# A causal filter and a spectral mix on one core: x two rows to a partition, the filter in twelve products per head on quarters of the array

## The chip, the cores and the metric

The kernel runs on one core of a Trainium2 chip. The metric is the device time of one execution in microseconds (us), of which the median over several runs is taken. The profile is of one further execution. Engines: TensorE (PE, with its weight loads PEld), VectorE (DVE), ScalarE (ACT), GpSimd (POOL) and SyncE (SP).

## The reference

`x` has 8 batches of 3264 rows and 192 channels. Eight heads of 24 channels each are filtered along the rows with a causal filter of 7 taps (a softmax of `weight`); the result is called c below. Of c the first 64 Fourier modes along the rows are taken, each is multiplied by a complex 192 x 192 matrix of its own, and they are transformed back to y. The output is u + relu(u @ w_ch) with u = c + y.

```python
out = np.einsum('hk,bskhg->bshg', softmax(weight), windows_of(x_pad))   # 7 taps, 8 heads of 24 channels
X = np.fft.rfft(c, axis=1)[:, :64]
Y = X @ (w_r + 1j * w_i)                                                # one matrix a mode
u = c + np.fft.irfft(Y, n=S, axis=1)
return u + np.maximum(u @ w_ch, 0)
```

Inputs and outputs are float32; x and the matrices are cast to bfloat16 while they are loaded.

## The kernel before, in words

**Layout.** The batches are taken in four pairs `q`. The 3264 rows of a batch are two halves of 1632; each half is six blocks (`NBH`) of 256 rows and a rest (`RR`) of 96. `xall[partition, q, t, k, d]` holds two tiles `t` of 128 rows to a block; row 128 t + p of a block lies on partition p, and `k` counts block, half and batch. `load_unit` (L169) issues one GpSimd transfer for each tile: 128 partitions, four rows of 192 float32 (768 B) each. `load_rest` (L179) loads the rests of all pairs, with some rows ahead of them.

**First stage.** A unit is one or two blocks of a pair: `UNITS` are blocks 4 and 5, blocks 2 and 3, and blocks 0 and 1 with the rest; the first pair has five smaller units (`UNITS0`). For a unit, `conv_pass` (L312) does the filter for two heads at a time: products of 128 rows of x (the moving side) with 64 columns of a band matrix (`band`, seen as `bd3`, one diagonal band of taps per head), which give every other row of c; `a` is the parity and `half` the tile. A second set of products adds the taps that reach into the tile or block before. The result, in a pair of PSUM banks from `next_pair` (three pairs in turn), is copied over x in `xall`, by ScalarE (three of four) or VectorE. So c lies with rows 2p + a of a block on partition p. A unit's filter also reads the block before its own, which the next unit loads.

`fold` (L348) makes the sum and the difference of the two halves on VectorE into `cpm`, and `dft` (L354) multiplies these with the table `ftab` (the cosines and sines, 128 columns) and adds up over the units of a pair in the bank `sums`. When a pair is done, `xtrans` (L372) transposes its spectrum into `xt`. The loop at L454 writes this order by hand: the filter of unit k, then the transform of unit k - 1, and in between one bank of transposes of c for the second stage (`some`, `c_bank`, L420: blocks of channels 0 to 127 of either batch, and channels 128 to 191 of both batches, each as a 64-wide transpose). After the loop come ten more such banks, the last transform, and the rest of the banks beside the mix. There are 42 banks (`tjobs`).

**The mix.** `mix` (L493) multiplies the spectrum of four modes at a time (`g`, 16 groups) with their matrices, on four column tiles of 32. The matrices come on GpSimd's queue behind x: groups 0 to 7 into places in `ct` that are still unused, groups 8 to 11 into `arena` when the filter's temporaries there are dead, groups 12 to 15 each into a place that the mix has just read (`load_w`, L299). The list at L827 (`beside`) says how many banks of transposes go beside each group; `beside_pair` puts some products of the second stage there, and `keep_busy` idle products.

**Second stage.** For each tile of 128 rows of c, `pieces` (L614) gives the products of either 64 rows of the array: three with the transposed c in `ct` (moving side `wa` and `wb`, halves of `w_ch`), and one with the inverse table `gtab` for y. `second_stage` (L743) plans them with fixed costs. ScalarE clamps, VectorE adds u, SyncE stores.

## Time and profile before

| | us |
|---|---|
| median of 3 runs | 175.84 (175.61 to 175.98) |
| the profiled execution | 175.52 |
| its span, first to last instruction | 173.7 |

| engine | busy us, share of the span | instructions |
|---|---|---|
| PE | 149.5 (86%) | 2837 |
| PEld | 127.8 (74%) | 2837 |
| DVE | 125.6 (72%) | 246 |
| ACT | 118.8 (68%) | 224 |
| POOL | 66.0 (38%) | 108 |

The transfers moved 40.85 MB, counted as they land. First come the loads of x and of the matrices on GpSimd's queue, at the end the stores on SyncE's. The mean granted clock of TensorE was 0.989.

How to read it: a row of a timeline has start and length in us, engine, line, operation, out<-in, shapes and count, and in brackets the idle time ahead of it with what ended it. A row of the windows has the stretch and its length, then busy time (and instructions) of PE, PEld, DVE, ACT and POOL, the granted clock, the DMA share and GB/s. A group has the count, then busy us and mean ns of one, then the idle time before. A wait has us in total, times, and the longest. A row of the transfers has their count, KB each and the median us from issue to landing.

### The profile page before, as it was taken

How to read it: one execution, taken by the hardware profiler on the slowest of the kernel's cores; microseconds unless marked ns; L12 is line 12 of the kernel's file. 1: busy time of each engine (PE TensorE's matmuls, PEld its weight loads, DVE VectorE, ACT ScalarE, POOL GpSimd, SP SyncE). 2: the span in 40 equal slices, each digit the busy share in tenths (PEclk: the TensorE clock that was granted, in tenths of full speed). 3: DMA queues.
4: the chain of work that ended last, by engine and by line, in shares of the span. 5: the costliest groups of instructions: out<-in, count | busy, mean ns of one | idle time of the engine just before them, and what ended most of it. 6: DMA issues, size and time to landing. Idle time of an engine off the chain costs nothing.

```text
span 173.7 us, 6647 instructions
## 1 busy us (share of the span) xinstructions
PE 149.5 (86%) x2837; PEld 127.8 (74%) x2837; DVE 125.6 (72%) x246; ACT 118.8 (68%) x224; POOL 66.0 (38%) x108
## 2 busy tenths in 40 slices
PE   0044898899999999799998899999999999999980
PEld 0043797789889889577865565788999988999950
DVE  3892868476778778675545542499998999999990
ACT  6369356658686686755874654588889899898850
POOL 7977997775775584344234300420000000000000
PEclk9999999999999999999999999999999999999995
DMA  2999999999999999999999996359969999999996
GB/s 17 166 173 189 193 188 191 191 189 192 191 190 191 192 204 206 206 206 206 207 208 206 207 205 115 88 191 389 388 233 396 351 357 383 337 339 385 386 356 196
DMA packets 51650, 40.85 MB, mean 235 GB/s; under 512 B 30020, under 2 KB 51524, under 8 KB 51620
## 3 DMA queue, kind: packets, MB, share of 16 engines
q0 software_dynamic: 36400, 20.06, 83.2%
q1 hardware_dynamic: 14948, 20.16, 32.5%
q8 instruction: 22, 0.36, 0.8%
q10 hardware_dynamic: 272, 0.20, 0.3%
q14 instruction: 8, 0.07, 0.1%
HBM read 39.62 MB, written 20.45 MB: 346 GB/s over the span
## 4 chain that ended last, share of the span: by engine, by line
DMA 46%; PE 37%; POOL 9%; issue 3%; DVE 1%; POOLq 0%; DVEq 0%
DMA xall<-in_x_dram 23%; PE outleft L644 18%; DMA arena<-in_moe_w_i_dram 13%; DMA ct<-in_moe_w_i_dram 11%; PE sumright L644 8%; PE mixright L644 8%; POOL xall L174 7%; DVE xall L712 1%; PE sumright L498 1%; PE trleft L429 1%; POOL loose L270 1%; PE sumright L818 0%; PE mixright L526 0%; PE mixright L548 0%; POOL arena L303 0%
## 5 line engine op out<-in xcount | busy, mean ns | idle before, releaser
L322 PEld LDWEIGHTS <-band 128*64 128x64 bf16 x944 | 38.7, 121 | 18.3 <-ACT band L241 11.1
L644 PEld LDWEIGHTS <-ct 64*128 64x128 bf16 x624 | 41.0, 94 | 4.8 <-PE trleft L644 0.5
L322 PE MATMUL cvleft<-xall,band 128*64 128x192 bf16 (+4 forms) x640 | 30.5, 248 | 13.9 <-ACT band L241 11.1
L644 PE MATMUL outleft<-mixa,gtab 64*128 64x384 bf16 x182 | 41.9, 323 | 0.1
L174 POOL DMA_DIRECT2D xall<-in_x_dram x48 | 36.0, 760 | 10.2 <-DMA xall<-in_x_dram 8.4
L644 PEld LDWEIGHTS <-gtab 64*128 64x128 bf16 x416 | 30.9, 94 | 3.0 <-PE outleft L644 1.1
L644 PE MATMUL outleft<-wa,ct 64*128 64x192 bf16 x208 | 30.4, 243 | 0.0
L351 DVE TENSOR_TENSOR arena<-xall 128x1536 bf16<-128x1536 bf16 (+1 forms) x28 | 22.4, 840 | 8.2 <-ACT xall L346 7.8
L690 ACT ACTIVATE outleft<-outleft 128x384 f32<-128x384 f32 x53 | 24.4, 477 | 4.6 <-PE outleft L644 2.3
L346 ACT CAST xall<-cvleft 128x768 bf16<-128x768 f32 (+3 forms) x29 | 21.4, 756 | 8.8 <-PE cvleft L322 7.3
L644 PE MATMUL sumright<-mixa,gtab 64*128 64x384 bf16 x92 | 25.8, 323 | 0.0
L644 PE MATMUL mixright<-mixa,gtab 64*128 64x384 bf16 x90 | 25.8, 323 | 0.0
L644 PE MATMUL outleft<-wb,ct 64*128 64x192 bf16 x104 | 23.3, 243 | 0.0
L398 DVE COPY ct<-trleft 128x1024 bf16<-128x1024 bf16 (+1 forms) x19 | 12.4, 662 | 12.7 <-PE trleft L429 7.8
L322 PE MATMUL cvright<-xall,band 128*64 128x192 bf16 (+4 forms) x304 | 15.9, 247 | 1.6 <-DVE xall L344 1.2
L396 ACT COPY ct<-trleft 128x1024 bf16<-128x1024 bf16 x13 | 13.2, 1012 | 4.6 <-PE trleft L426 2.4
L712 DVE TENSOR_TENSOR arena<-outleft,xall 128x384 f32<-128x384 f32 x27 | 14.4, 553 | 2.5 <-PE outleft L644 2.1
L346 ACT CAST xall<-cvright 128x768 bf16<-128x768 f32 (+3 forms) x13 | 9.8, 751 | 8.4 <-PE cvright L322 6.1
L644 PE MATMUL sumright<-wa,ct 64*128 64x192 bf16 x88 | 14.2, 243 | 0.0
L644 PE MATMUL mixright<-wa,ct 64*128 64x192 bf16 x80 | 13.8, 243 | 0.0
L426 PEld LDWEIGHTS <-xall 128*128 128x128 bf16 x208 | 11.7, 98 | 2.6 <-issue 0.3
L690 ACT ACTIVATE sumright<-sumright 128x384 f32<-128x384 f32 x26 | 12.3, 477 | 1.4 <-PE sumright L644 0.3
(147 smaller groups left out, 283.2 us busy)
## 6 DMA issues: line engine op xcount, KB each, us to landing
xall<-in_x_dram POOLq DMA_DIRECT2D x48, 192.0 KB, 7.9
out_dram<-arena SPq DMA_DIRECT2D x23, 384.0 KB, 4.0
out_dram<-xall SPq DMA_DIRECT2D x13, 384.0 KB, 4.1
out_dram<-ct SPq DMA_DIRECT2D x8, 384.0 KB, 4.6
ct<-in_moe_w_r_dram POOLq DMA_DIRECT2D x8, 288.0 KB, 9.4
ct<-in_moe_w_i_dram POOLq DMA_DIRECT2D x8, 288.0 KB, 10.4
arena<-in_moe_w_r_dram POOLq DMA_DIRECT2D x8, 288.0 KB, 10.5
arena<-in_moe_w_i_dram POOLq DMA_DIRECT2D x8, 288.0 KB, 10.9
```

The source lines that it names most:

```text
L174: nc.gpsimd.dma_start(out=xall[:, q, t % 2, k:k + 4, :], in_=src)
L270: nc.gpsimd.affine_select(out=dst, in_=dst, compare_op=ALU.not_equal, fill=fill, base=base, pattern=pattern, channel_multiplier=1)
L322: nc.tensor.matmul(o, bd3[:, h, c0:c0 + P - 1:2], xall[:, q, t, ks:ks + n, GRP * h:GRP * h + GRP], start=(main and a == 0), stop=not main, ...
L346: nc.scalar.copy(out=dst, in_=srcv)
L351: nc.vector.tensor_tensor(out=cpm[:, r, :, 0:2 * nb, :], in0=src[:, :, :, 0, :], in1=src[:, :, :, 1, :], op=op)
L396: nc.scalar.copy(out=out, in_=in_)
L398: nc.vector.tensor_copy(out=out, in_=in_)
L426: nc.tensor.transpose(o, cv[:, blk, 0:P], ident[:])
L429: nc.tensor.transpose(o[64 * i:64 * i + 64, :], cv[:, i, P:D], ident[:], tile_position=(0, 64 * i))
L644: m = nc.tensor.matmul((Z[s % NZ] if bank is None else bank)[:, cols], l, r, start=start, stop=stop, skip_group_check=True)
L690: act = nc.scalar.activation(out=z, in_=z, func=ACT.Relu)
L712: add = nc.vector.tensor_tensor(out=o[:, :, a, :], in0=Z[s % NZ][:, 0:2 * D].rearrange("p (i d) -> p i d", i=2), in1=c_rows(q, kk)[:, a, : ...
```

## The change

**x in memory.** x comes two rows to a partition: rows 2p and 2p + 1 of a block lie on partition p, next to each other, `xall[partition, q, k, t, d]` with `t` now the parity. A transfer is one half of one block of both batches, 128 partitions with two pieces of two rows (1536 B). The number of these transfers stays 48 of 192 KB; the rest's four shrink to 48 partitions for each pair. Rows that the filter needs ahead of the rest are moved from the last block by `rows_ahead`: four small products with a shift matrix (`ahead`) and four copies for each pair, ahead of its first unit.

**The filter.** `conv_head` does one head of a unit in one of six single banks (`next_bank`), in three steps of four products on the four 64 x 64 quarters of the array: equal parities (both at once, twice as wide), then odd into even, then even into odd. The products from the lower 64 rows are issued at once, those from the upper 64 rows six steps (two heads) later, after a `nop` that waits for the head's last lower product; then the bank is copied, by VectorE for heads 4 and 6, else by ScalarE. The band matrix has two parities of 129 columns per head. All pairs now have the three units of `UNITS`.

**The order.** `fold` of the unit before comes after head 1 of a unit; its transform after head 7. There are no transposes for the second stage in the filter's loop: the eight banks move beside the mix (`beside`).

**Second stage.** c of both batches lies side by side (`call`), so the transposes are three full blocks of 128 channels for two batches. Where 64 channels now lie on the other half of the partitions than in `wa`, their products use `wc`, `wa` with its halves swapped: two ScalarE copies ahead of the mix.

```diff
-    UNITS0 = ((5, 1, 0), (4, 1, 0), (3, 1, 0), (1, 2, 0), (0, 1, 1))
     UNITS = ((4, 2, 0), (2, 2, 0), (0, 2, 1))
-    units = [(q,) + u for q in range(NQ) for u in (UNITS if q else UNITS0)]
+    units = [(q,) + u for q in range(NQ) for u in UNITS]
...
+    call = xall[:, :, :, :, :].rearrange("p q (n i) t d -> p q n (i t d)", i=2).rearrange(
+        "p q n (t i d) -> p q n t i d", t=2, i=2)
...
-    cz = hand_out("left", "cv", (2, 2))
+    cz = hand_out("left", "cv", (1, 1, 1, 1))
...
-    cz += hand_out("right", "cv", (2,))
+    cz += hand_out("right", "cv", (1, 1))
...
+                k = 2 + 4 * b + 2 * h
+                src = bass.AP(tensor=x.tensor, offset=x.offset + (2 * q * S + HS * h + 2 * P * b) * D,
+                              ap=[[2 * D, P], [S * D, 2], [1, 2 * D]])
+                nc.gpsimd.dma_start(out=xall[:, q, k:k + 2, :, :].rearrange("p k t d -> p k (t d)"), in_=src)
...
+    def rows_ahead(q):
+        k = 2 + 4 * (NBH - 1)
+        for i in range(2):
+            z = next_bank()
+            for h in range(2):
+                nc.tensor.matmul(z[64 * (1 - h):64 * (1 - h) + R0, 0:2 * D], ahead[P - 32:P, :],
+                                 xall[P - 32:P, q, k + 2 * h + i, :, :].rearrange("p t d -> p (t d)"), start=True,
+                                 stop=True, tile_position=(P - 32, 64 * (1 - h)), skip_group_check=True)
+            for h, engine in enumerate((nc.scalar.copy, nc.vector.tensor_copy)):
+                r = slice(64 * (1 - h), 64 * (1 - h) + R0)
+                engine(out=xall[r, q, i, :, :].rearrange("p t d -> p (t d)"), in_=z[r, 0:2 * D])
+
+    LAG = 6
+    upper = []
+    def flush(n=0):
+        while len(upper) > n:
+            upper.pop(0)()
+
+    def conv_head(q, b0, nb, rest, h):
+        z = next_bank()
+        nk = 4 * nb + 2 * rest
+        k0 = 2 + 4 * b0 - 2 * rest
+        cols = slice(GRP * h, GRP * h + GRP)
+        xq = xall[:, q, :, :, cols].rearrange("p (n i) t e -> p t n i e", i=2)
+        last = []
+        def put(src, dst, c, a, b, base, k, back, start=False, stop=False):
+            r, o = slice(64 * src, 64 * src + 64), z[64 * dst:64 * dst + 64, 0:2 * GRP * nk]
+            return nc.tensor.matmul(o.rearrange("p (n a i e) -> p a n i e", a=2, i=2, e=GRP)[:, a, (k - k0) // 2:, :, :],
+                                    bd3[r, h, base + c:base + c + 64],
+                                    xq[r, b, (k - back) // 2:(k0 + nk - back) // 2, :, :], start=start, stop=stop,
+                                    tile_position=(64 * src, 64 * dst), skip_group_check=True)
+        def later(step, *args):
+            if step == 0:
+                nop = nc.tensor.nop()
+                tc.add_manual_dep(nop.ins, last[-1], ...)
+            put(1, 1, 0, *args, k0, 0, stop=step == 2)
+            put(1, 0, 64, *args, max(k0, 4), 4, stop=step == 2)
+            if step == 2:
+                dst = call[:, q, k0 // 2:(k0 + nk) // 2, :, :, cols].rearrange("p n t i e -> p n (t i) e")
+                srcv = z[:, 0:2 * GRP * nk].rearrange("p (n v e) -> p n v e", v=4, e=GRP)
+                if h in (4, 6):
+                    nc.vector.tensor_copy(out=dst, in_=srcv)
+                else:
+                    nc.scalar.copy(out=dst, in_=srcv)
+        both = slice(0, 2)
+        for step, args in enumerate(((both, both, 0), (0, 1, PB - 1), (1, 0, PB))):
+            put(0, 1, 64, *args, k0, 0, start=step == 0)
+            last.append(put(0, 0, 0, *args, k0, 0, start=step == 0).ins.name)
+            upper.append(lambda step=step, args=args: later(step, *args))
+            flush(LAG)
...
-            if blk < 2:
-                nc.tensor.transpose(o, cv[:, blk, 0:P], ident[:])
-            else:
-                for i in range(2):
-                    nc.tensor.transpose(o[64 * i:64 * i + 64, :], cv[:, i, P:D], ident[:],
-                                        tile_position=(0, 64 * i))
+            nc.tensor.transpose(o, cv.rearrange("p i d -> p (i d)")[:, P * blk:P * blk + P], ident[:])
...
     for k, u in enumerate(units):
+        if u[1] + u[2] == NBH:
+            rows_ahead(u[0])
+        for h in range(H):
+            conv_head(*u, h)
+            if k == 0 and h in (2, 4):
+                table(h // 2 - 1)
+            if h == 1 and prev is not None:
+                fold(*prev)
+                if k == 1:
+                    table(2)
         if pend is not None:
             xtrans(pend)
             pend = None
-        conv_pass(*u, 2)
-        if k > len(UNITS0):
-            some([next_pair()[:, 0, :]])
-        conv_pass(*u, 3)
         if prev is not None:
             dft(*prev)
...
+    flush()
+    lt += hand_out("left", "tr", (1, 1, 1, 1))
+    trans_banks(2)
+    fold(*prev)
...
-                    for blk, w, i in ((0, wa, 0), (1, wa, 1), (2, wb, row))]
+                    for blk, w, i in (((0, wa, 0), (1, wc, 1), (2, wb, 1)) if row else
+                                      ((0, wa, 0), (1, wb, 0), (2, wc, 1)))]
...
-    for g, beside in enumerate((0, 1, 1, 2, 2, 2, 1, 2, 2, 2, 2, 2, 2, 2, 0, 0)):
+    for i in range(2):
+        nc.scalar.copy(out=wc[64 * i:64 * i + 64, :], in_=wa[64 * (1 - i):64 * (1 - i) + 64, :])
+    for g, beside in enumerate((1, 2, 2, 2, 2, 2, 2, 3, 3, 3, 3, 3, 2, 2, 0, 0)):
```

138 lines of the change are left out of this document (50 added, 88 removed).

## The prediction

> **What bounds the kernel now.** I read the end of the first stage first, then went back along it: the chain of waits, the list of waits, TensorE's timeline, the windows.
>
> ```profile
> 91.62 10.57 DMA arena<-in_moe_w_i_dram
> 102.23 0.46 PE sumright L498 x11
> ```
> ```profile
> PEld L498 <- DMA arena<-in_moe_w_i_dram: 3.0, 6, 1.0
> ...
> PE sumright L498 <- DMA arena<-in_moe_w_i_dram: 1.7, 4, 0.7
> ```
> ```profile
> 87.73 0.46 PE L498 MATMUL sumright<-arena,mixa 128*16 128x192 bf16 x12
> ...
> 99.37 0.47 PE L498 MATMUL sumright<-arena,mixa 128*16 128x192 bf16 x12 [0.20 <-DMA arena<-in_moe_w_i_dram]
> ...
> 102.23 0.46 PE L498 MATMUL sumright<-arena,mixa 128*16 128x192 bf16 x12 [0.30 <-DMA arena<-in_moe_w_i_dram]
> ...
> 105.10 0.46 PE L498 MATMUL sumright<-arena,mixa 128*16 128x192 bf16 x12
> ...
> 107.97 0.46 PE L498 MATMUL sumright<-arena,mixa 128*16 128x192 bf16 x12
> ```
>
> The chain reaches the mix at 102.23 through a weight transfer, and the mixes come 2.86 to 2.87 us apart. The windows and the transfers' sizes say why:
>
> ```profile
> 0.00:10.00 10.00, 0.00 (x0) 0.00 (x0) 6.43 (x31) 4.63 (x5) 8.86 (x18) 1.00 0.93 100
> 10.00:20.00 10.00, 6.15 (x132) 5.62 (x134) 6.14 (x19) 6.97 (x17) 7.50 (x14) 1.00 1.57 186
> 20.00:30.00 10.00, 8.90 (x216) 8.23 (x214) 7.52 (x14) 5.82 (x10) 9.11 (x15) 1.00 1.60 191
> ...
> 50.00:60.00 10.00, 10.00 (x214) 9.01 (x211) 7.73 (x10) 6.75 (x9) 6.03 (x11) 1.00 1.56 190
> ...
> 80.00:90.00 10.00, 10.00 (x232) 7.82 (x227) 5.33 (x11) 7.36 (x13) 3.66 (x6) 1.00 1.21 206
> ```
> ```profile
> xall<-in_x_dram POOLq DMA_DIRECT2D x48, 192.0 KB, 7.9
> ...
> ct<-in_moe_w_r_dram POOLq DMA_DIRECT2D x8, 288.0 KB, 9.4
> ...
> xall<-in_x_dram POOLq DMA_DIRECT2D x4, 168.0 KB, 7.8
> ```
>
> 288 KB at 206 GB/s is 1.43 us, and one group of modes is two such transfers: 2.86 us. So from 99 us on the mixes go at the pace of the loads, which follow x on one queue without a pause, and TensorE waits 1.7 us for them in all. But TensorE is close behind: the convolution ends near 69.5 and the mix at 87.73 follows work that had no wait. The first stage has two limits almost equally near, the queue and TensorE. After 107.97 comes the second stage, whose products keep count, sizes and planner; only which half of an item's columns is written first differs, and the third weight tile that this needs is two short copies on ACT at the start of the mix, beside the transposes. I carry its 65.8 us over unchanged.
>
> **The loads.** An x transfer is 192 KB in 512 pieces of 384 B (as landed), a weight transfer 288 KB in 256 of 1152 B. At 190 and 206 GB/s over 16 engines these are 32.3 and 89.5 ns a piece; the line through both gives 60.9 ns for the new 768 B piece. An x transfer becomes 16 x 60.9 = 0.97 us instead of 1.035: 48 save 2.9 us. The four transfers of the rest shrink from 168 to 144 KB: 0.7 us. In all 3.6 us, so that the last weights land near 104.4. Bounds: 0.5 us (rate stays 190, only the rest's bytes go) and 4.6 us (x at 206). The Trainium skill (DMA: Bandwidth & Descriptors, Specifications) asks for pieces of 512 B or more for line rate, and 384 B lies under that. The traced gap between 384 and 1152 B, 8% per byte, is all that this rule can bring here; no run here shows 768 B.
>
> GpSimd still issues 48 transfers of x, each with half the pieces:
>
> ```profile
> L174 POOL DMA_DIRECT2D xall<-in_x_dram x48 | 36.0, 760 | 10.2 <-DMA xall<-in_x_dram 8.4 <-POOLq L877 0.8 <-issue 0.6
> ```
>
> Its 36.0 us wait mostly for older transfers to land, so a cheaper issue is worth nothing by itself.
>
> **The convolution's products.** A head's unit of two blocks is now three steps on four quarters, of 384, 192 and 192 columns each. What does a quarter cost? The mix runs on four column tiles, the old convolution on two:
>
> ```profile
> 77.70 0.71 PE L498 MATMUL sumright<-ct,mixa 128*16 128x192 bf16 x24 [0.17 <-ACT mixa L389]
> ```
> ```profile
> L498 PE MATMUL sumright<-ct,mixa 128*16 128x192 bf16 x96 | 3.5, 257 | 0.2 <-ACT mixa L389 0.2
> ...
> L366 PE MATMUL sumright<-arena,ftab 128*64 128x384 bf16 x96 | 11.4, 335 | 1.2 <-DVE arena L351 1.2
> ```
> ```profile
> 43.38 1.07 PE L322 MATMUL cvright<-xall,band 128*64 128x192 bf16 x16
> ...
> 45.70 0.62 PE L426 MATMUL cvright<-ident,xall 128*128 128x128 bf16 x8
> 46.25 0.85 PE L322 MATMUL cvleft<-xall,band 128*64 128x192 bf16 x16
> 46.93 0.82 PE L366 MATMUL sumright<-arena,ftab 128*64 128x384 bf16 x8
> 47.58 0.49 PE L366 MATMUL sumright<-xall,ftab 128*64 128x384 bf16 x4
> 47.91 0.83 PE L322 MATMUL cvleft<-xall,band 128*64 128x192 bf16 x16
> ...
> 56.55 1.52 PE L322 MATMUL cvleft<-xall,band 128*64 128x192 bf16 x32
> ```
>
> (0.71 - 0.257) / 23 = 19.7 ns a product: 80 ns for 192 columns on a tile, four at once. So a head costs 160 + 80 + 80 = 0.33 us and, with the rest, 960 columns or 0.41 us. Per pair of batches: 8 x (2 x 0.33 + 0.41) = 8.5 us. Added to it: the transforms, 3 x 0.65 (46.93 to 47.58) and 0.33, together 2.3; the transposition of the sums, 0.4; `rows_ahead`, four products of 384 columns in two pairs, 0.32; and changes of tile shape. A bank of eight transposes took 0.55 us (45.70 to 46.25) where its columns need 0.43, so a change is about 0.1 us; six per pair and one for `rows_ahead` are 0.7. With 0.2 us where heads of two widths meet, that is 12.4 us. Before, a pair took 13.2 us (43.38 to 56.55) with three banks of transposes (1.7 us) that are now moved behind.
>
> **Waits that it adds.** These are my own estimate from the copies' lengths:
>
> ```profile
> L351 DVE TENSOR_TENSOR arena<-xall 128x1536 bf16<-128x1536 bf16 x20 | 18.3, 954 | 7.4 <-ACT xall L346 7.4
> ...
> L346 ACT CAST xall<-cvleft 128x768 bf16<-128x768 f32 x15 | 11.7, 802 | 4.8 <-PE cvleft L322 3.3 <-DMA xall<-in_x_dram 1.5
> ...
> L344 DVE CAST xall<-cvleft 128x768 bf16<-128x768 f32 x4 | 3.8, 957 | 2.2 <-PE cvleft L322 1.7 <-DMA xall<-in_x_dram 0.5
> ...
> L346 ACT CAST xall<-cvleft 128x384 bf16<-128x384 f32 x6 | 2.7, 474 | 1.8 <-PE cvleft L322 1.7
> ...
> L344 DVE CAST xall<-cvleft 128x384 bf16<-128x384 f32 x2 | 1.1, 558 | 0.5 <-PE cvleft L322 0.4
> ```
>
> A copy of 384 is 0.47 us on ACT, 0.56 on DVE; between the rows, 480 is 0.56 and 0.66. ACT then has about 11 us a pair and DVE as much (two folds of 0.95 in each unit among them): neither is full. But the order has tight places. A head keeps its bank until its last products, two heads later, are copied, so of six banks three are always open. Times are from a unit's start.
> - First unit of a pair: DVE must copy both results of `rows_ahead` (from 0.5 to 1.5 us) before it copies head 6 of the unit before (to 2.1 us). Head 2 needs that bank at 1.35: TensorE, and all that is queued behind, waits 0.8 us.
> - Second unit: the transposition of the sums takes the banks of heads 2 and 3, whose copies ACT ends at about 3.1 us behind head 7 of the unit before; wanted at 2.8: 0.3.
> - Third: head 6 of the second unit is copied at 1.2 us, its bank wanted at 0.8: 0.4.
> - A fold (1.9 us on DVE) cannot start before head 7's copy at 1.5 us, and its transform is wanted at 3.4: just hidden; any further delay shows there.
>
> Together 1.5 us, so 13.9 us a pair; bounds 0 and 3 us (all three places doubled). The added `nop` stands in TensorE's order before a head's upper products, and holds up all behind it until that head's last lower product is done; that one was issued a head (0.33 us) before and lasts 0.26: met.
>
> **Start of the run.** Now the third unit of the first pair needs 16 x transfers and the rest: 3.74 MB. The windows give 2.86 MB by 20 us and 0.191 MB per us: 24.6, less 1.3 for longer pieces. Landings are noticed later than the bytes say:
>
> ```profile
> 29.82 0.63 PE L322 MATMUL cvright<-xall,band 128*64 128x192 bf16 x8
> 30.91 0.52 PE L322 MATMUL cvright<-xall,band 128*64 128x192 bf16 x8 [0.46 <-DMA xall<-in_x_dram]
> ```
>
> This wait, for 24 transfers (4.62 MB, by the windows 29.2), ended 1.7 us later. So 25.0 us, then that unit (3.7) and a transform with its changes (0.9): the second pair begins at 29.6, as before (29.82). From there the loads run ahead. The edits at the start (larger band copies, fewer masks, `rows_ahead`, big first units in place of small ones) cost nothing while the first two units end by 25.0. They can start their upper products once 8 transfers are there, near 14, but TensorE is slow at first:
>
> ```profile
> 21.64 1.49 PE L322 MATMUL cvleft<-xall,band 128*64 128x96 bf16 x32 [0.55 <-DVE xall L344]
> ```
>
> 32 products of 96 columns at 40 ns, as long as 192 columns take later: half speed. At half speed 16 heads are 10.5 us, which ends at 24.5; without that cover the excess would count in full, 1 us if the slow time lasts and ACT's tables hold up two banks.
>
> **The sum.** Convolution flushed: 29.6 + 3 x 13.9 + 0.3 = 71.6 us. From there to the last mix is TensorE work:
>
> ```profile
> 70.08 0.97 PE L429 MATMUL trleft<-ident,xall 128*64 128x128 bf16 x28 [0.41 <-ACT xall L346]
> ...
> 82.34 1.07 PE L426 MATMUL trleft<-ident,xall 128*128 128x128 bf16 x16
> 83.33 0.46 PE L498 MATMUL sumright<-ct,mixa 128*16 128x192 bf16 x12
> ```
>
> It took 7.6 us from 70.08 to the first mix; with the fold ready a little sooner, 7.0. From 77.70 to 87.73 were 10.0 us with 11 banks of transposes beside the mixes; two banks take 0.99 (82.34 to 83.33), and 16 now make it 12.5. From 87.73 to 107.97 were 20.2 us, paced by loads; four steps now have a third bank (0.5 each), of which 1.7 us fit into the old waits and 0.4 us drop with the last leftover bank: 20.1. Sum 39.6; last mix at 111.2, 3.2 us later than 107.97. The loads (104.4) would allow 3.6 us earlier. The profiled time is 175.52 us for a span of 173.7; 178.7 profiled, and with the median of the runs 0.3 above the profile, 179.0 us.
>
> **The rivals.**
> - *The waits do not come, and the loads set the end.* At 12.4 us a pair the flush is at 67.1, the last mix at 106.7: 174.6 us. If the mix phase also finds cover for its transposes, the limit is the landing at 104.4: 172.3. For it: both engines that copy have room. Against it: the order above. It is faster than now where a pair falls below 12.8 us.
> - *Quarters do not start that closely.* The 19.7 ns row has weights of 16 columns, the quarters 64. With a product each 28 ns, the two narrow steps last 112 instead of 80 ns: 0.06 x 16 + 0.08 = 1.0 us a pair, 3.1 in all: 182.1 us. For it: no row here shows 64-column weights at under 28 ns for long. By the skill's floor of about 25 ns from start to start (TensorE: Matmul & The Clock Gate, Part 1) it would be 1.7 us; the mix row, at 19.7, disagrees with that floor.
> - *Only two quarters at once.* 8.5 us more a pair: about 204.5. Nothing speaks for it but that no row here has four such quarters.
> - *The loads get no faster.* Then they land at 107.4, which leaves my forecast alone and takes the first rival's gain down to 0.5 us.
>
> **How the numbers follow.** Forecast (own range 177 to 181, waits of 0.8 to 2.2 us a pair) 0.50; first rival 0.33; start distance 0.08; two at once 0.03; between, within 0.35 us of now, 0.06. 0.2% of 175.8 is 0.35 us, about what a measurement of this kernel can tell. Faster 0.33, same 0.06, slower 0.61. The range 173.2 to 182.2 leaves out the best end of the first rival, two at once, and the tail of the start distance.
>
> **What would show it.** Right: L322's successor with four products in about 82 ns; TensorE idle for DVE and ACT in the first unit of a pair; a pair near 13.9 us; mixes no longer ending waits for weights. Wrong: mixes still 2.87 us apart with the last at 104 to 105, or a pair at 12.5; or a head near 0.4 us, which is the start distance.

## The result, and the profile after

The changed kernel is slower: 183.55 us median (182.53 to 183.64, 4 runs) against 175.91 (175.61 to 176.73, 4 runs), ratio 1.0413, 95% interval 1.0363 to 1.0464. The forecast was 179.0 with a range up to 182.2. The sign was right; the loss is 7.6 us instead of 3.1, and most of what is missing comes from a limit that the prediction did not have. The ranges below are of all runs of a kernel; one run each of rows_xtrans_loop_late, loads_four and paced_four was over 1.5% slower than the fastest of its kernel, and nothing rests on it.

The page of the changed kernel (profiled execution 183.64 us): the engine totals, the chain's shares, the filter's weight loads, and the queue that brings instructions.

```profile
PE 154.8 (85%) x2957; PEld 123.6 (68%) x2957; DVE 128.6 (71%) x257; ACT 125.7 (69%) x264; POOL 65.0 (36%) x108
PE 75%; DMA 8%; DVE 6%; POOL 4%; issue 3%; ACT 1%; POOLq 0%; DVEq 0%
L357 PEld LDWEIGHTS <-band 64*64 64x64 bf16 x1152 | 33.6, 110 | 22.6 <-issue 18.7
q8 instruction: 23, 0.38, 0.8%
```

TensorE now makes three quarters of the chain (75%, where the transfers keep 8%), and no mix waits for weights: where the chain of before went through a matrix transfer at 91.62, GpSimd now waits for the mix before it may load.

```profile
POOL arena L314 <- PE sumright L527: 18.7, 4, 13.5
PE cvleft L357 <- DVE xall L373: 2.8, 5, 1.1
PE cvright L357 <- issue: 1.8, 3, 0.8
PE cvleft L357 <- issue: 0.9, 1, 0.9
```
```profile
84.09 0.46 PE L527 MATMUL sumright<-ct,mixa 128*16 128x192 bf16 x12
95.94 0.46 PE L527 MATMUL sumright<-arena,mixa 128*16 128x192 bf16 x12
115.43 0.46 PE L527 MATMUL sumright<-arena,mixa 128*16 128x192 bf16 x12
```

The last mix is at 115.43, 7.46 us later than before (107.97). Windows cut at the starts of the second, third and fourth pair of batches, at the end of the filter, the first mix and the last show where it came from. First the kernel before, then the changed one; the counts behind PE and PEld are TensorE's products and weight loads.

```profile
29.82:43.38 13.56, 12.44 (x264) 11.18 (x262) 9.01 (x12) 8.55 (x12) 8.84 (x12) 1.00 1.59 191
43.38:56.55 13.17, 13.15 (x275) 11.69 (x272) 10.25 (x12) 9.29 (x13) 9.06 (x14) 1.00 1.60 190
56.55:70.08 13.53, 13.12 (x290) 11.65 (x284) 10.15 (x12) 9.80 (x13) 8.15 (x14) 1.00 1.29 201
70.08:77.70 7.62, 6.76 (x114) 5.58 (x113) 5.97 (x10) 4.57 (x7) 2.95 (x6) 1.00 1.21 206
77.70:107.97 30.27, 28.54 (x577) 20.24 (x577) 14.74 (x29) 18.60 (x33) 8.47 (x14) 1.00 1.14 196
107.97:173.70 65.73, 60.65 (x991) 53.79 (x990) 55.50 (x111) 50.60 (x118) 3.09 (x6) 0.97 0.89 316
```
```profile
10.00:20.00 10.00, 7.13 (x132) 5.46 (x136) 6.46 (x23) 8.78 (x21) 7.23 (x12) 1.00 1.31 200
28.42:44.21 15.79, 13.21 (x333) 9.37 (x333) 10.38 (x15) 10.07 (x22) 13.17 (x20) 1.00 1.27 191
44.21:59.72 15.51, 13.35 (x334) 9.73 (x332) 10.32 (x15) 9.89 (x22) 10.76 (x18) 1.00 1.30 200
59.72:75.31 15.59, 13.37 (x334) 9.66 (x332) 10.32 (x15) 10.08 (x22) 7.17 (x12) 1.00 1.21 206
75.31:84.09 8.78, 7.62 (x118) 6.27 (x116) 6.13 (x9) 4.67 (x7) 3.06 (x5) 1.00 1.22 208
84.09:115.43 31.34, 31.30 (x562) 23.64 (x562) 18.35 (x35) 22.16 (x39) 4.93 (x8) 1.00 0.77 128
115.43:181.80 66.37, 60.65 (x991) 53.82 (x990) 55.52 (x111) 50.60 (x118) 3.08 (x6) 0.97 0.88 313
```

Against before: the second pair begins 1.40 us earlier (28.42 for 29.82), the three pairs take 46.89 us for 40.26 (+6.63, with eight banks of transposes gone from them), then +1.16, +1.07 and +0.64. Together 8.10, which is the difference of the spans. So the question is the pair: 15.63 us on average, where 13.9 was forecast.

TensorE's timeline inside the filter shows two kinds of stop:

```profile
42.80 0.22 PE L357 MATMUL cvleft<-xall,band 64*64 64x144 bf16 x1 [0.92 <-issue]
46.73 0.35 PE L357 MATMUL cvright<-xall,band 64*64 64x384 bf16 x2 [1.10 <-DVE xall L373]
55.22 0.35 PE L357 MATMUL cvright<-xall,band 64*64 64x384 bf16 x2 [0.74 <-issue]
56.38 0.39 PE L357 MATMUL cvright<-xall,band 64*64 64x480 bf16 x2 [0.33 <-DVE xall L373]
72.99 0.29 PE L357 MATMUL cvright<-xall,band 64*64 64x240 bf16 x2 [0.80 <-issue]
```

Those for `DVE xall L373` (VectorE's copies) are the waits for a bank that the prediction had, in the first and third unit of a pair. Those with `issue` have no releaser. They come at 36.48, 42.80, 55.22, 66.97 and 72.99; the differences are 6.32, 12.42, 11.75 and 6.02, all near multiples of 6.1 us. Counted along the trace, each falls on a TensorE instruction whose number is 193 modulo 256, and a 16384 B packet of the instruction queue (256 instructions of 64 B; the page has 23 packets of together 0.38 MB) had started 2.3 to 2.9 us before.

### The profile page after: what moved, and what is told of

Same layout as the page of the kernel before. It is cut to its first block, busy times and chain, and to the rows that moved or that the text cites. A ratio compares the mean times of both kernels' runs of the same rounds, so it can differ in the third digit from the quotient of the medians.

```text
span 181.8 us, 6942 instructions
## 1 busy us (share of the span) xinstructions
PE 154.8 (85%) x2957; PEld 123.6 (68%) x2957; DVE 128.6 (71%) x257; ACT 125.7 (69%) x264; POOL 65.0 (36%) x108
## 4 chain that ended last, share of the span: by engine, by line
PE 75%; DMA 8%; DVE 6%; POOL 4%; issue 3%; ACT 1%; POOLq 0%; DVEq 0%
PE outleft L674 17%; PE cvleft L357 11%; PE trleft L460 10%; PE sumright L674 8%; DMA xall<-in_x_dram 8%; PE mixright L674 7%; PE cvright L357 5%; PE sumright L402 5%; POOL xall L182 4%; PE sumright L527 4%; PE trleft L674 2%; DVE xall L373 2%; DVE xall L334 2%; PE mixright L555 1%; DVE xall L742 1%
## 5 line engine op out<-in xcount | busy, mean ns | idle before, releaser
L357 PE MATMUL cvleft<-xall,band 64*64 64x192 bf16 (+4 forms) x768 | 42.6, 285 | 7.5 <-DVE xall L373 2.8
L357 PEld LDWEIGHTS <-band 64*64 64x64 bf16 x1152 | 33.6, 110 | 22.6 <-issue 18.7
L357 PE MATMUL cvright<-xall,band 64*64 64x192 bf16 (+4 forms) x384 | 29.3, 285 | 4.2 <-issue 1.8
L375 ACT CAST xall<-cvleft 128x384 bf16<-128x384 f32 (+1 forms) x48 | 22.7, 515 | 10.3 <-PE cvleft L357 6.2
L674 PE MATMUL sumright<-mixa,gtab 64*128 64x384 bf16 x92 | 25.8, 323 | 0.0
L674 PE MATMUL mixright<-mixa,gtab 64*128 64x384 bf16 x90 | 25.8, 322 | 0.0
L387 DVE TENSOR_TENSOR arena<-xall 128x1536 bf16<-128x1536 bf16 x24 | 22.0, 959 | 2.4 <-ACT xall L375 1.9
L674 PE MATMUL outleft<-wb,ct 64*128 64x192 bf16 x104 | 23.1, 243 | 0.0
L674 PE MATMUL outleft<-wa,ct 64*128 64x192 bf16 x104 | 22.9, 243 | 0.0
L674 PE MATMUL outleft<-wc,ct 64*128 64x192 bf16 x104 | 21.7, 243 | 0.0
L460 PE MATMUL trleft<-ident,xall 128*128 128x128 bf16 x312 | 20.2, 219 | 0.7 <-ACT xall L375 0.7
L375 ACT CAST xall<-cvright 128x384 bf16<-128x384 f32 (+1 forms) x24 | 11.4, 509 | 8.1 <-PE cvright L357 4.0
L742 DVE TENSOR_TENSOR arena<-outleft,xall 128x384 f32<-128x384 f32 x27 | 14.4, 554 | 2.5 <-PE outleft L674 2.1
L373 DVE CAST xall<-cvleft 128x384 bf16<-128x384 f32 (+1 forms) x16 | 9.3, 584 | 7.1 <-ACT loose L406 2.9
```

The source lines that it names most:

```text
L357: return nc.tensor.matmul(o.rearrange("p (n a i e) -> p a n i e", a=2, i=2, e=GRP)[:, a, (k - k0) // 2:, :, :], bd3[r, h, base + c:base + ...
L373: nc.vector.tensor_copy(out=dst, in_=srcv)
L375: nc.scalar.copy(out=dst, in_=srcv)
L387: nc.vector.tensor_tensor(out=cpm[:, r, 0:nb, :, :, :].rearrange("p b t i d -> p b (t i d)"), in0=src[:, :, 0, :], in1=src[:, :, 1, :], op=op)
L460: nc.tensor.transpose(o, cv.rearrange("p i d -> p (i d)")[:, P * blk:P * blk + P], ident[:])
L674: m = nc.tensor.matmul((Z[s % NZ] if bank is None else bank)[:, cols], l, r, start=start, stop=stop, skip_group_check=True)
```

## The experiments

Two theories stood against each other. *Supply:* TensorE runs out of instructions, which come in chunks of 256. *Banks:* copies and banks set the pair, and the rest only fills their time. A third, plain TensorE work wherever it stands, is tested with them.

**1. Do the stops belong to a place in the stream?** (shift64: 64 tiny products ahead of the loop)

```diff
+    for i in range(64):
+        c0 = 32 * (i % 4)
+        nc.tensor.matmul(cz[5][c0:c0 + R0, 0:16], ahead[P - 32:P, :], ahead[P - 32:P, :], start=True, stop=True,
+                         tile_position=(P - 32, c0), skip_group_check=True)
     for k, u in enumerate(units):
```

> The changed kernel with 64 tiny products (16 columns) put on TensorE ahead of the filter's loop, in the time before the first x has landed; nothing else. In the changed kernel TensorE stops with no releaser ('issue') at 36.48, 42.80, 55.22, 66.97 and 72.99 us, 0.3 to 1.2 us each, always at a TensorE instruction whose number is 193 modulo 256, and each time a 16384 B packet of the instruction queue had started 2.3 to 2.4 us before. Theory instruction fetch: the stops belong to the place in the instruction stream, so they move to products that stand 64 earlier in the code (about 1.3 us earlier inside a unit), while the numbers stay 193 modulo 256; their sum stays between 2 and 5 us, the time between 181.5 and 185.5. Rival theory, the nops or the quarters themselves (a wait of the head's upper products for its lower ones): the stops stay at the same heads of the same units, and the time is 183.5.

183.16 us (182.78 to 183.77). Its timeline:

```profile
40.39 0.32 PE L357 MATMUL cvleft<-xall,band 64*64 64x384 bf16 x1 [1.08 <-issue]
46.89 0.35 PE L357 MATMUL cvright<-xall,band 64*64 64x384 bf16 x2 [1.10 <-DVE xall L373]
52.99 0.52 PE L357 MATMUL cvleft<-xall,band 64*64 64x192 bf16 x10 [1.17 <-issue]
```

The wait for VectorE stays at its head (46.89 for 46.73). Three of the stops without a releaser (42.80, 55.22 and 72.99) come 2.2 to 2.5 us earlier, where 1.3 was expected, at other products, and are again at instructions 193 modulo 256; at the place of the other two TensorE now stops for less than 0.2 us. They belong to the stream, not to the filter's products or its `nop`.

**2. The supply alone.** (fetch_alone: 1024 of these tiny products instead of 64; fetch_late: the same 1024 beside mix 13, when the loads are all but over)

> The changed kernel with 1024 tiny products (2048 TensorE instructions, no memory traffic of their own, no waits) ahead of the filter's loop. In shift64, 64 of them were issued in 0.47 us, 7.5 ns each, so 256 instructions would take 0.96 us if they were there. This measures the disputed cost alone. Theory instruction fetch: after the first 500 to 700 instructions, which are there when the kernel starts, TensorE stops at each instruction 193 modulo 256, and a chunk of 256 takes about as long as a fetch, 2.0 to 2.5 us; 2048 take 12 to 16 us in all, each stop ending 2.2 to 2.5 us after a 16384 B packet started. Rival (the stops belong to the filter's own products or its nops): all are issued in about 7.7 us without a stop. The run's time is worse by what of this exceeds the wait for the first x; it is not the point.

> The same 1024 tiny products as in fetch_alone, but beside mix 13 (about 112 us), when at most the last two groups of weights are still being loaded, instead of ahead of the loop, where x is loaded all the time. In fetch_alone a 16384 B packet of instructions starts 3.6 to 3.9 us after the chunk before it is begun and ends 2.2 to 2.5 us ahead of its own use. Theory A, the instructions queue behind the loads: without loads the packet starts at once and a chunk of 256 takes about 2.3 to 4 us (before_more_instr has one of 3.73 at 89.98, when its loads were over). Theory B, the supply has a fixed pace: 5.9 to 6.2 us here too. The time is 20 to 45 us above the changed kernel and not the point.

TensorE's timeline of fetch_alone, then of fetch_late:

```profile
11.79 1.17 PE L487 MATMUL cvright<-ahead 32*16 32x16 bf16 x128 [4.18 <-issue]
17.99 1.16 PE L487 MATMUL cvright<-ahead 32*16 32x16 bf16 x128 [5.03 <-issue]
23.91 1.16 PE L487 MATMUL cvright<-ahead 32*16 32x16 bf16 x128 [4.76 <-issue]
```
```profile
116.07 1.17 PE L890 MATMUL sumright<-ahead 32*16 32x16 bf16 x128 [2.30 <-issue]
120.08 1.17 PE L890 MATMUL sumright<-ahead 32*16 32x16 bf16 x128 [2.83 <-issue]
123.53 1.17 PE L890 MATMUL sumright<-ahead 32*16 32x16 bf16 x128 [2.28 <-issue]
```

128 products with their weight loads are 256 instructions: done in 1.17 us, then nothing until the next chunk. A chunk comes each 5.92 to 6.20 us while x is loaded (201 GB/s) and each 3.45 to 4.01 us almost without loads (5 GB/s). The granted clock was 1.00 in the first and 0.55 in the second, but the 128 products take 1.17 us in both. The expectation of fetch_alone had the right kind of stop, the first at instruction 449 instead of after 500 to 700, and the wrong size (2.0 to 2.5 us a chunk): it took the 2.3 us from a packet's start to the next chunk for the whole of it. In the trace the packet starts only 3.6 to 3.9 us after the chunk before was begun, and 1.0 to 1.7 us after in fetch_late. So the supply is 23.7 ns an instruction under these loads (6.06 us over 256), and a pair of 666 instructions is 15.8 us by it alone; measured are 15.51 to 15.79. This is an estimate and no floor: in the runs of experiment 5 a chunk that TensorE waited for came after 5.5 us too (41.65 in rows_xtrans_in_sums). Here the Trainium skill (Runtime: NRT & Kernel Launch, Instruction fetch mechanics) has the blocks of 256 instructions and that the next is fetched while one is executed, and calls the cost of a block's end mostly hidden, since instructions are dispatched more slowly than they come; these runs agree on the blocks and not on the cost.

**3. The count of instructions, up and down.** (split_sixteen: the equal parities one after the other, sixteen products a head of the same columns. no_carry: the product out of the block before left out, so that the first rows of a block lack taps; nine a head. no_carry_banks: that with freed banks, see 5)

```diff
-        for step, args in enumerate(((both, both, 0), (0, 1, PB - 1), (1, 0, PB))):
+        for step, args in enumerate(((0, 0, 0), (1, 1, 0), (0, 1, PB - 1), (1, 0, PB))):     # split_sixteen, LAG = 8
...
-            put(1, 0, 64, *args, max(k0, 4), 4, stop=step == 2)                                # no_carry
```

> The changed kernel with sixteen products a head instead of twelve: the equal parities one after the other (192 columns each) instead of both in one product of 384; the same columns, result and tile shape. TensorE instructions rise from 667 to 859 a pair. Theory instruction supply: 859 x 23.7 ns = 20.4 us a pair instead of 15.6, 14 us in three pairs and 2 to 4 in the first: 197 to 202 us, stops of 2 us with no releaser at each instruction 193 modulo 256. Rival, TensorE's columns, banks and copies set the pair: products of 192 columns start every 20.5 ns on four quarters as they do now, so 183 to 185 us.

> The changed kernel with nine products a head instead of twelve, all on 64x64 quarters: the product from the upper 64 rows of the block before into the lower 64 rows is left out (so the first rows of each block of 128 partitions lack some taps; the time is what is wanted). The quarters work side by side, so the columns of a head last as long as before (0.33 us by the busiest quarter); TensorE instructions fall from 667 to 523 a pair. Theory instruction supply (256 in about 6.06 us, 23.7 ns each): 15.8 us a pair becomes 12.4, so TensorE's work with its bank waits (12.6 + 1.7 us) sets the pair, 14.0 to 14.5: 3.3 to 5 us less in the three pairs, 178.5 to 180.5 us. Rival, banks and copies set the pair and the stops for instructions only fill their time: 15.3 to 15.6, 182.5 to 183.5 us.

> no_carry with the banks of rows_xtrans_in_sums (same part of the filter left out). With the full filter these banks were worth 0.8 us of 182.8 to 183.6. Theory instruction supply: with the supply out of the way they count: a pair at 13.0 to 13.6 (12.6 and up to 0.8 for VectorE's fold), 2 to 3 us under no_carry, 175.5 to 178 us, near the kernel before. Rival: as little as before, under 1 us below no_carry.

Windows of the second and third pair of split_sixteen, and then of no_carry:

```profile
33.08:52.21 19.13, 14.95 (x430) 11.55 (x428) 10.51 (x15) 10.30 (x22) 14.10 (x21) 0.90 1.30 197
52.21:73.24 21.03, 15.50 (x430) 11.99 (x428) 10.32 (x15) 10.15 (x22) 11.56 (x19) 0.92 1.24 205
```
```profile
28.91:43.29 14.38, 13.00 (x262) 9.54 (x261) 10.32 (x15) 9.92 (x22) 11.45 (x18) 1.00 1.22 177
43.29:57.67 14.38, 13.00 (x262) 9.45 (x261) 10.32 (x15) 9.89 (x22) 9.19 (x14) 1.00 1.29 192
```

858 instructions take 19.13 and 21.03 us (22.3 and 24.5 ns each). The granted clock was 0.90 and 0.92 there, which may be part of the longer busy time (14.95 and 15.50 us for 13.2 to 13.4). The rest is stops: the chunks begin 5.6 to 6.6 us apart, with up to 3 us from one product's start to the next. In no_carry 523 take 14.38, with no stop without a releaser left in the filter and the waits for VectorE unchanged (1.10 and 0.3 us idle). The runs: split_sixteen 199.72 us (198.91 to 199.84), no_carry 180.31 (180.09 to 181.67), no_carry_banks 177.45 (177.19 to 178.01), each median inside what the supply theory gave. With the supply out of the way freed banks are worth 2.9 us; with twelve products a head they had been worth 0.8 (experiment 5).

**4. The same in the kernel before.** (before_more_instr: a product of 16 columns behind each product of the old filter, from the second pair on)

> The kernel before, with one tiny product of 16 columns (its result, in unused columns of the bank, is not read) behind each product of the filter in the second to fourth pair of batches: twice as many TensorE instructions there. In the kernel before, 256 instructions last about 5.2 us in the filter, each fetch starts 80 to 160 instructions ahead of its chunk, and TensorE stops there only once, for 0.13 us (67.63). The tiny products make the products' distance 41 + 8 to 20 ns, so four instructions last about 50 to 60 ns. Theory instruction fetch: stops with no releaser of 0.3 to 1.3 us appear at instructions 193 modulo 256, five to eight of them between 30 and 80 us, in the kernel's old order and on halves of the array. Rival, quarters or nops: no such stop, only the tiny products' own time, 2 to 4 us a pair. Time 183 to 194 us either way; the stops decide.

198.76 us in one run, above the 183 to 194 expected; the stops were longer, too, up to 2 us instead of 1.3. They appear in the old order and on halves of the array:

```profile
42.55 0.17 PE L327 MATMUL cvright<-xall,band 128*64 128x16 bf16 x1 [1.91 <-issue]
49.00 0.20 PE L327 MATMUL cvright<-xall,band 128*64 128x16 bf16 x1 [0.71 <-issue]
55.17 0.28 PE L322 MATMUL cvleft<-xall,band 128*64 128x192 bf16 x2 [1.64 <-issue]
```

They are 6.45 and 6.17 us apart. So the limit is not of the quarters. The kernel before ran just inside it: 526 to 574 instructions a pair are 12.5 to 13.6 us of supply, and its pairs took 13.17 to 13.56. In its trace a chunk lasts 5.6 to 6.5 us there, and not the 5.2 of the expectation.

**5. Banks and order, with the supply as it is.** (rows_in_sums: `rows_ahead` into the idle bank of `sums`, copied at the unit's end; rows_xtrans_in_sums: one bank of `xtrans` there too; trans_in_loop: eight banks of transposes in the filter's loop; rows_xtrans_loop: both; rows_xtrans_loop_late: and the transform of a unit after head 0 of the next unit but one)

```diff
-            z = next_bank()                                    # rows_ahead
+        z = sums[q % 2]                                        # products to partitions 64 * (1 - h) + 32 * i
...
-        z = [next_bank() for i in range(2)]                    # xtrans
+        z = [next_bank(), sums[q % 2] if q < NQ - 1 else next_bank()]
...
+            if h == 5 and k > 3:                               # trans_in_loop
+                some([next_bank()])
-    for g, beside in enumerate((1, 2, 2, 2, 2, 2, 2, 3, 3, 3, 3, 3, 2, 2, 0, 0)):
+    for g, beside in enumerate((0, 1, 1, 2, 2, 2, 1, 2, 2, 2, 2, 2, 2, 2, 0, 0)):
```

> The changed kernel, but rows_ahead writes its four products into the spectrum's idle bank (four column tiles, one bank) instead of two of the six banks of the filter, and its copies come at the end of the unit, ahead of the transform. Theory banks: the stop of 1.25 us in the first unit of the second, third and fourth pair (30.94, 46.73, 62.24, for VectorE's copy of head 6) goes, and some 0.2 us of TensorE with it: each of the three pair starts lies 1.2 to 1.4 us closer, 3.5 to 4 us in all, 180 us. Theory instruction fetch adds: the chunk whose boundary lies later in the first unit had been fetched during that stop; without it TensorE stops there for up to 1 us per pair with no releaser, so the gain is 1 to 2.5 us, 181 to 182.5. Rival, the copies are simply too slow for twelve products a head (VectorE and ScalarE bound): another wait for a copy of the same size comes a few heads later, 183.5.

> As rows_in_sums, and the transposition of the sums takes one bank of the filter and the idle spectrum bank instead of two banks of the filter. Theory banks: the stop of 0.3 to 0.5 us in the third unit (39.76, 56.38, 70.98, for head 6's copy) goes as well: 1 to 1.5 us less than rows_in_sums, 178.7 to 180.5 us with it. Instruction fetch: part of it comes back as stops with no releaser; those then make up nearly all that TensorE waits inside the filter, 1 to 2 us a pair. Rival, copy engines bound: no change against rows_in_sums.

> The changed kernel with eight banks of transposes put back into the filter's loop (one per unit from the fifth unit on, after head 5) and the list beside the mix as in the kernel before. The 64 transposes last 54 ns each with two instructions, against 20.5 ns for a product on a quarter, so a chunk of 256 instructions lasts longer where they stand. Theory instruction fetch: the stops with no releaser shrink or go in the units concerned, 1.5 to 3 us gained, which come through to the end if TensorE alone paces the rest: 180.5 to 182 us, with a pair at 16.0 to 16.4 us and the first mix to last mix at 27.5. Theory plain TensorE work (the sum of the products sets the end wherever they stand): 183.5. Rival, banks: each bank of transposes takes one of the six filter banks and its copy of 0.7 to 1.0 us delays the heads behind it, 0.5 us a unit: 186 us or more.

> rows_xtrans_in_sums and trans_in_loop together: banks for rows_ahead and the transposition taken out of the filter's six, eight banks of transposes in the loop. In rows_xtrans_in_sums (profiled span 179.8) the stops with no releaser cost about 5 us beyond the normal start distance (0.6 to 1.6 us, seven times), in trans_in_loop one was left of them, but waits for banks (three of 1.36, four of 0.55, one of 0.81) remained. Theory fetch and banks together: both kinds go, the transposes in the loop cost nearly nothing since they lie where TensorE stood still, 177 to 179 us. Theory plain TensorE work: as rows_xtrans_in_sums, 181 to 183. Rival, the transposes' own copies now make the banks late: 182 or more.

> rows_xtrans_loop, and the transform of a unit comes a whole unit and a head later (after head 0 of the unit after the next's start) instead of at the end of the next unit. In rows_xtrans_in_sums TensorE waits 0.62 to 1.0 us for VectorE's fold at the transform in the first unit of a pair (35.65, 46.84, 61.84); that wait goes: 1.5 to 2 us less than rows_xtrans_loop, 175 to 177.5 us. If instruction fetch is what then ends the stretch, the gain is under 0.7 us. Rival: the later fold of the last units makes the end of the filter later by as much, no gain.

Measured: 181.98 (181.18 to 182.84), 182.77 (181.58 to 183.42), 183.75 (183.46 to 184.52), 185.34 (184.81 to 186.49) and 182.03 us (181.83 to 185.24). Only the first is inside its main expectation (181 to 182.5, banks and supply together); the others lie 1.8 to 6.3 us above theirs. 183.75 us is also what plain TensorE work gave for trans_in_loop (183.5), but that theory can't hold: with the same columns a pair takes 19.13 to 21.03 us in split_sixteen and 14.40 in loads_four. In rows_xtrans_in_sums the waits for a bank at a pair's start and in its third unit are gone (one of 0.80 us is left, at 35.65), and stops without a releaser stand at most chunks instead; its second and third pair:

```profile
28.50:43.05 14.55, 13.07 (x333) 9.78 (x332) 10.40 (x15) 9.93 (x22) 12.74 (x19) 1.00 1.29 191
43.05:58.06 15.01, 13.41 (x335) 10.03 (x334) 10.32 (x15) 9.69 (x22) 10.03 (x17) 1.00 1.31 200
```

Their 665 and 669 instructions are 21.9 and 22.4 ns each, less than the 23.7 of fetch_alone: the chunks begin 5.4 to 6.2 us apart.

The pairs of trans_in_loop have 699 and 716 instructions and take 16.35 and 16.54 us, 23.1 to 23.4 ns each. This would explain a miss: I had expected the transposes to fill the stops, 1.5 to 3 us gained. Where the supply sets the pace they only add 16 instructions a bank, and nothing was gained. rows_xtrans_loop is slower than either of its parts (pairs of 17.73 and 17.08 us). Its chunks begin 6.0 to 6.4 us apart there, most of them after a stop; why those of trans_in_loop came sooner, 5.7 us apart on average, stays open.

**6. Fewer instructions at the same work.** (merged_nine: the two products that read the lower 64 rows made one of 64 rows by 128 columns; merged_banks and merged_banks_late: with 5's edits)

```diff
-            put(0, 1, 64, *args, k0, 0, start=step == 0)
-            last.append(put(0, 0, 0, *args, k0, 0, start=step == 0).ins.name)
+            last.append(put(0, None, 0, *args, k0, 0, start=step == 0).ins.name)   # band columns base to base + 128
```

> The changed kernel with nine products a head instead of twelve: the two quarters of the lower 64 rows read the same x and neighbouring columns of the band, so they become one product of 64 rows by 128 columns. Columns streamed and arithmetic are the same; TensorE instructions fall by 48 a unit, from 667 to 523 a pair of batches. fetch_alone showed 256 instructions in 5.92 to 6.20 us when nothing else limits, 23.7 ns an instruction, and a pair of the changed kernel is 667 instructions, 15.8 us, against 15.63 measured. Theory instruction supply sets the pair: 523 instructions are 12.4 us, so TensorE's own work (12.6) and the bank waits (1.7) take over: a pair at 14.2 to 14.6, 3 to 4.3 us off the run, 179 to 180.5 us, stops with no releaser gone or under 0.3 us. Rival, bank waits alone (the supply is only a symptom of a late start): 183. Rival, a 64x128 tile does not run beside the two 64x64 tiles of the other rows: a head takes half as long again, 17 us a pair, 188 us.

> merged_nine with the banks of rows_xtrans_in_sums. There the freed banks were worth only 1 us a run since the stops for instructions came in their place (14.55 and 15.0 us a pair for 662 instructions). Theory instruction supply: now the freed banks count in full, 1.3 to 1.7 us a pair less the wait for VectorE's fold that showed there (0.6 to 1.0): a pair at 13.2 to 13.7, 176.5 to 178.5 us. Rival, copies and banks never mattered: as merged_nine.

> merged_banks with the transform of a unit after head 0 of the unit after the next's start, so that it does not wait for the fold. Theory: the wait of 0.6 to 1.0 us in a pair's first unit goes, a pair at 12.5 to 13.0 us, 174 to 176.5 us, about the kernel before (176.0) or under it; the last mix then comes at 105 to 107.5 us, near the landing of the last weights. Rival: the supply of instructions binds again beside the mix (476 instructions in 11.85 us there, 24.9 ns each), and what the filter gains is partly lost there: 176.5 to 178.5.

345.41, 344.61 and 343.21 us: far outside all that was expected. The timeline of merged_nine shows where the time goes:

```profile
30.09 0.37 PE L357 MATMUL cvright<-xall,band 64*64 64x192 bf16 x2
30.39 0.34 PE L357 MATMUL cvleft<-xall,band 64*128 64x192 bf16 x1
30.66 0.37 PE L357 MATMUL cvright<-xall,band 64*64 64x192 bf16 x2
30.97 0.50 PE L357 MATMUL cvleft<-xall,band 64*128 64x384 bf16 x1
31.40 0.53 PE L357 MATMUL cvright<-xall,band 64*64 64x384 bf16 x2
```

At each change between a tile of 64x128 and tiles of 64x64 the next product starts only when the one before is nearly at its end: 0.27 and 0.30 us from start to start for 192 columns, where twelve products on equal quarters take 0.33 us for the whole head. For 384 columns it is 0.43 us (30.97 to 31.40). So 192 more columns cost 0.16 us, twice the 0.08 of the changed kernel, though the granted clock reads 1.00; that leaves an estimated 0.11 to 0.14 us for the change itself. Why the columns run at half speed is not shown. The Trainium skill (TensorEngine Tiling (Array Packing), Key Properties) says that a change of the tiling mode drains the engine; this trace agrees, as products on either side of a change hardly overlap. My rival for this run, half as long again for a head, was far too small, since it left the products pipelined. Of the supply these three runs say nothing.

**7. Do the loads slow the supply in the kernel itself?** (loads_four: a load is issued when the fourth ahead of it has landed; paced_four and paced_five: this with four or five in flight for x of the second to fourth pair only, with the freed banks and the late transform of 5, without transposes in the loop)

```diff
+        if q and len(loads) >= 5:            # loads_four: every load, 4
+            tc.add_manual_dep(inst.ins, loads[-5], ..., reason="few loads in flight")
+        loads.append(inst.ins.name)
```

> The changed kernel, but a load of x or of a matrix is issued only when the fourth load ahead of it has landed, so four are in flight instead of seven or eight (issue to landing 7.4 us for x). Everything else as it was. Theory A, the instruction packets queue behind the loads in flight: their start comes 1.5 to 2.5 us earlier in a chunk, a chunk takes 4 to 5 us when wanted, TensorE's work and bank waits (14.4 us in no_carry) set the pair instead of the supply (15.6): 3 to 4 us less, 179.5 to 181 us, if four in flight keep the loads at 0.98 us each; if they slow to 1.2 us, x lands 10 us later and half of it is lost. Theory B, fixed pace: the pair stays at 15.5 to 15.8, 183 to 184.5 us.

> The changed kernel with three edits: the banks of rows_xtrans_in_sums; the transform of a unit after head 0 of the unit after the next's start (as in rows_xtrans_loop_late, without its transposes); and x of the second to fourth pair loaded with four in flight, the first pair and the matrices as they were. loads_four showed 14.40 us a pair, the same as no_carry, so the supply of instructions no longer bound; what it lost lay in the slower loads ahead of the second pair (28.4 became 33.1 us) and of the matrices. Theory: second pair at 28.4 to 28.9, a pair at 12.7 to 13.6 (TensorE's work, or 12 loads of 1.1 to 1.2 us), flush at 67 to 70, first mix 7.8 later, last mix 31.3 after that: 174.5 to 178 us, about the kernel before (176). Rival, four in flight are not few enough when TensorE asks for 256 instructions each 5 us: pairs at 14.5 to 15, 179 to 181.5 us.

> paced_four with five in flight. Loads nearer to 0.98 us each, instruction packets queued behind one more load. Theory: if the loads' pace bound paced_four, 0.5 to 2 us less than it; if the supply binds, a pair at 13.5 to 15, 1 to 4 us more than it.

Windows of the second and third pair, of loads_four and then of paced_five:

```profile
33.12:47.52 14.40, 13.01 (x336) 9.73 (x334) 10.32 (x15) 9.93 (x22) 10.05 (x19) 1.00 1.10 154
47.52:61.91 14.39, 13.00 (x335) 9.64 (x333) 10.32 (x15) 9.90 (x22) 7.93 (x12) 1.00 1.16 160
```
```profile
28.62:42.57 13.95, 13.30 (x334) 9.81 (x333) 10.52 (x17) 9.80 (x23) 10.33 (x20) 1.00 1.12 158
42.57:56.37 13.80, 13.35 (x336) 9.78 (x334) 10.01 (x16) 9.77 (x22) 9.68 (x14) 1.00 1.26 178
```

What TensorE waits for in the filter of loads_four is VectorE, as in the changed kernel:

```profile
PE cvleft L365 <- DVE xall L381: 2.9, 5, 1.1
PE cvright L365 <- DVE xall L381: 1.4, 2, 1.1
```

With the full filter and all its instructions loads_four has the pair of no_carry, 14.40 us for 14.38. Its time is 191.31 us (189.35 to 192.70) all the same, for its loads move 154 to 160 GB/s instead of 200: the second pair starts at 33.12 instead of 28.42, and mixes wait for matrices again (3.6 us in five waits). The changed kernel itself agrees at one place: from 30 to 34 us, when its loads move 182 GB/s, the packet at 33.56 starts 2.0 us after the chunk before was begun, and the later ones of the filter 3.4 to 3.9 us after. paced_four, 184.07 us (182.64 to 186.55), missed: its x came late too, and TensorE waits up to 1.80 us for it. paced_five is 178.31 us (178.27 to 178.34), ratio 1.0132 (1.0072 to 1.0193) to before: 5.2 us better than the changed kernel, and still 1.3% above the kernel before. What of the 5.2 us is the loads' pace and what the freed banks and the late transform was not separated. Four stops for instructions are left in its last three pairs (0.4 to 1.1 us from start to start). Whether it is the number of loads in flight or the bytes per microsecond that hold the instructions up was not separated; both fell. No version was found that beats both kernels.

## Why the prediction was right or wrong

**Right.** The loads: 200 GB/s from 10 to 20 us, where before had 186, and x lands every 0.98 us (forecast 0.97). The quarters run four at once at full rate: 384-column products of consecutive heads start at 50.03, 50.38, 50.71 and 51.03, 0.33 us a head. Mixes no longer wait for weights. The second stage gives 66.37 us for 65.8. And, nearly, TensorE's pair without the supply: 14.38 to 14.40 us in no_carry and loads_four, for 13.9. From start to start the waits for banks are 1.9 of it (1.36 in the first unit for 0.8, none in the second for 0.3, 0.55 in the third for 0.4; 1.5 in all was forecast), and the other 12.5 are TensorE's work, for 12.4. The idle times of the rows (1.10 and 0.29) are shorter, since the product ahead of a stop counts as busy until its end. In the first unit VectorE's copies of `rows_ahead` wait for ScalarE's (three times in the changed kernel, 3.7 us in all), which the prediction had side by side; no run shows how much of the longer wait that is.

**Wrong: the step "13.9 us a pair".** It added columns, tile changes and waits for copies, and bounded the waits by copies alone. The term that is missing is the count of instructions. 666 in 13.9 us are 20.9 ns each; in the kernel before the densest ten microseconds shown, 80 to 90 us, have 459 (21.8 ns each), and its pairs were at 23.6 to 25.8. The pair cost 15.63: 0.5 us over the forecast mostly by longer waits for banks (14.4), and 1.2 more by the supply of instructions, which loads_four takes away without leaving out any; in three pairs 5.2. The rows of the prediction's own windows had the counts; I read only their busy times. The sign does not hang on the missing term: no_carry, without its stops, is still at 180.31 us.

**The other terms.** The second pair starts at 28.42, for 29.6: the landing of the rest is noticed at 24.12 and not 25.0, and what follows takes 4.3 us for 4.6. From the end of the filter's loop to the first mix it is 8.78 us instead of 7.3:

```profile
75.31 1.00 PE L357 MATMUL cvleft<-xall,band 64*64 64x480 bf16 x12
76.97 2.39 PE L460 MATMUL trleft<-ident,xall 128*128 128x128 bf16 x40 [0.66 <-ACT xall L375]
```

The last twelve products of the filter and the wait for their copy take 1.66 us, to 76.97. The prediction had 0.3 for it, as its 7.6 us of before began at 70.08, behind such a wait. From there to the first mix it is 7.12 us, for 7.0. First to last mix 31.34 for 32.6. These three come to -1.2, +1.5 and -1.3; with +0.6 of the second stage and +5.2 of the pairs that is the 4.9 us between 178.7 and the profiled 183.64, but for rounding. That the four smaller ones nearly cancel is luck.

**The rivals.** "Waits do not come, loads set the end" fell, as the waits came. "Quarters do not start that closely" had 182.1 us, nearest to the result, and is wrong: they start 20.5 ns apart (0.33 us for sixteen times 192 columns). Its own sum is a little short, too: two narrow steps at 112 for 102 ns are 0.16 us for the eight heads of the third unit, not 0.08. What it priced by the product comes by the chunk. "The loads get no faster" fell. The range ended 1.35 us short because no case had a limit other than columns, copies and loads.

## What to carry to other kernels

When an edit splits TensorE's work into more and shorter products, count its instructions in each stage (both counts of a windows row) and divide the stage's time by them; if the result is below what any stage of the profile has kept up for 10 us, the supply of instructions is a rival with a price. An idle time whose releaser is "issue" and that comes at a steady distance is the mark of it, and shifting the stream by a known number of instructions, or changing their count at equal work, tells it from a wait of the code. While the supply is the limit, freeing banks or filling the stops with other products brings little: each fills the other's time.

## What the runs showed of the hardware that was not expected

- TensorE's instructions came in chunks of 256 (16384 B): one each 5.92 to 6.20 us while loads ran at some 200 GB/s, 3.45 to 4.01 us at 5 GB/s, though the 128 tiny products of a chunk, with their weight loads, were done in 1.17 us. They started within 0.99 us, 7.8 ns a product.
- With a change between 64x128 and 64x64 tiles at each product, products of 192 columns started 0.27 to 0.30 us apart, of which 0.16 us are columns at half speed, and the kernel's time nearly doubled (345.41 us for 183.55).
- With 768 B pieces x came at 200 GB/s from 10 to 20 us, where 384 B pieces had 186; 192 KB landed each 0.98 us.
